# A new order of the engines' instruction streams, searched with other transfer times, in a fused linear-attention and gated-FFN layer

## The chip, the cores and the metric

The kernel runs on one core of a Trainium2 chip. The metric is the device time of one execution in microseconds (us). A core has a matrix engine (PE; its weight loads are listed apart as PEld), three engines for elementwise work (DVE, ACT, POOL), and SP, which in this kernel issues DMA transfers alone. Each engine runs its own instruction stream in the order in which it was written; between engines, semaphores make an instruction wait for what it needs.

## The reference

One layer for 2048 tokens of width 640, in bf16: linear attention with 32 heads of 20 on a layer-normed input, a residual, then a gated FFN without a nonlinearity on the layer-normed sum, a residual.

```python
def _A_ref(x, wqkv, w_phi, wo):
    qkv = (x @ wqkv).reshape(B, S, 3, H, Dh)  # to q, k, v per head
    pq = jnp.einsum("bhsd,hdf->bhsf", q, w_phi)
    pk = jnp.einsum("bhsd,hdf->bhsf", k, w_phi)
    phi_q = jnp.concatenate([_softmax(pq), _softmax(-pq)], axis=-1)
    phi_k = jnp.concatenate([_softmax(pk), _softmax(-pk)], axis=-1)
    kv = jnp.einsum("bhsf,bhsd->bhfd", phi_k, v)
    z  = jnp.einsum("bhsf->bhf", phi_k)
    num = jnp.einsum("bhqf,bhfd->bhqd", phi_q, kv)
    den = jnp.einsum("bhqf,bhf->bhq", phi_q, z)[..., None] + 1e-6
    return (num / den).reshape(B, S, D) @ wo

def _B_ref(x, w_gate, w_up, w_down):        # F = 1536
    return ((x @ w_gate) * (x @ w_up)) @ w_down

h = x + _A_ref(_layernorm(x), A_wqkv, A_w_phi, A_wo)
h2 = h + _B_ref(_layernorm(h), B_w_gate, B_w_up, B_w_down)
```

## The kernel before, in words

The 2048 tokens are 16 tiles of 128 (numbers 0 to 15 in the names below), and four blocks of four tiles for the FFN. The program is a list of operations, each of which belongs to a named unit:

- `in`, `lT*`, `lx*`, `lwq`, `lwo`, `lg`, `lu`, `ld`: loads of x (transposed, L553, and plain, L549) and of the weights. `ld` is the load of w_down, 1.92 MB, into the space (vaug) that held the values.
- `wk`, `x*`, `wv`, `c*`, `wm`, `wq*`, `y*`: the weights of keys, values and queries are centred and multiplied with w_phi. For the keys, PE turns w_k in five pieces (L746), ACT (L803) and DVE (L806) copy the last turn out with the mean (DVE L775) taken off, and PE multiplies with the block matrix Phi (which DVE's and POOL's L636 build) in five units, x0 to x4.
- `s0, s2, s4, s8, s12`: sums and sums of squares of a batch of tokens for the layer norm (PE with 129 columns, DVE L698 and L702, POOL L707 to L718).
- `k*` and `K*`: scores of a tile of keys (PE), their maximum (DVE L925, L928), two exponentials (ACT L933), sums and reciprocals (DVE L947, L949), and the softmax product (POOL L950).
- `v*`: values (PE, ACT L956). `A*` and `Aout`: kv, summed over all tiles in PSUM, and its copy (DVE L1037, L1040).
- `q*` and `Q*`: the same for a tile of queries, with three buffers `eq` for the exponentials. Four exponentials (two for the first tiles), DVE L987 and L993, POOL L994 and L999, and then SP issues two transposing loads (L553) of the tile into phiqT, the first half of five pieces of 128 columns and the second of six. A buffer of `eq` is free for a later tile when both halves have landed.
- `n*`: numerators and denominators of a tile (PE), the division (DVE L1073, L1075) and the transposing of the result. `h*`: times wo, the residual and the second norm.
- `f b.ft.j`: one of twelve tiles of F, for block b: in the first block two products on PE, two copies by ACT (L1139, L1143) and a multiplication on POOL (L1145); in the later blocks a scheme with seven half products instead of eight (L1210), where PE goes on with a PSUM tile that ACT (L1220) or DVE (L1235, L1237) has copied in between.
- `d*` and `D*`: the down projections, the residual (DVE L1342) and the store.

What an engine does after what is not found by a scheduler at run time or at build time. `ORDER` (L74 and following) holds for each of the five engines a list of unit names, and each name takes the next operation of that unit on that engine. `Prog.place()` walks the five lists at once with a model of the time of each operation (`t`: how long it holds its engine, `lat`: until its result can be used, `size`: a transfer's time on the DMA engines), takes at each step the operation that can start first, and gives out PSUM buffers (four of two banks, `ps`), the three `eq` buffers and the slots of the DMA rings in that order. `finish()` then writes the semaphore waits. The model's times thus don't run on the chip; they decide which buffer number an operation gets and in which order buffers come free, and they are what the lists were searched with.

Of the kernel before, what the change touches and what calls it, by code (L numbers as in the profile page):

```python
# [11 lines left out]
P = 128  # L12
S = 2048
D = 640
NT = S // P
NC = D // P
# [81 lines left out]
    "DVE":  # L98
# [16 lines left out]
    "ACT":  # L115
# [318 lines left out]
def _build(ctx, nc, A_x, A_wqkv, A_w_phi, A_wo, B_w_gate, B_w_up, B_w_down, out):  # L434
    g = Prog(nc, ctx)
# [8 lines left out]
    x_all = sb([P, NT, D], BF16, "x_all")  # L444
# [186 lines left out]
    for a in range(NC):  # L631
        lo, hi = CH[a]
        n = hi - lo + 1
# [866 lines left out]
```

## Time and profile before

| | |
|---|---|
| median of three runs | 267.84 us (267.67, 267.84, 268.10) |
| the profiled execution | 267.55 us |
| its span, first to last instruction | 265.8 us |
| mean granted clock of PE | 0.999 |
| instructions PE, DVE, ACT, POOL | 2418, 417, 387, 243 |
| DMA moved in the span | 28.65 MB |

The profile page gives the busy time of each engine, the span in slices, the chain of waits that ended last, and groups of instructions by line; the trace behind it answers for any window. A row of a timeline is: start in us, length in us, engine, line, operation, output and inputs with their shapes, how many in a row, and in brackets the idle time ahead and what ended it. The end of a matmul is modelled, so rows of PE overlap a little.

### The profile page before, as it was taken

What the parts mean: (1) busy time and instruction counts of PE and PEld (TensorE: products, weight loads), DVE (VectorE), ACT (ScalarE), POOL (GpSimd) and SP (SyncE); (2) the same over time, 40 slices, a digit from 0 to 9 for tenths busy, and PEclk for the clock granted to TensorE, in tenths of its full rate; (3) what the DMA queues carried; (4) which work ended last, traced back from release to release, by engine and by line L of the source; (5) the groups of instructions that cost most, each with busy time, mean ns of one, the idle gap of its engine ahead of it and who ended that gap; (6) DMA issues with size and microseconds to landing.
All of it is one profiled execution on the core that took longest, in us unless ns stands there. A gap on an engine that the chain in (4) does not pass through costs nothing.

```text
span 265.8 us, 6243 instructions
## 1 busy us (share of the span) xinstructions
PE 260.4 (98%) x2418; PEld 200.0 (75%) x2433; DVE 222.7 (84%) x417; ACT 177.2 (67%) x387; POOL 190.1 (72%) x243
## 2 busy tenths in 40 slices
PE   8999999999999999999999999999999999999995
PEld 8877777776877787777767887777777777777773
DVE  1999999999999876998999778988778788675683
ACT  2567999999857998769553695764857555645220
POOL 5446989999932889999974789359866575648652
PEclk9999999999999999999999999999999999999999
DMA  7997999903155789666856515300410401001012
GB/s 188 302 138 175 165 233 401 382 32 75 39 82 100 89 247 210 130 106 133 131 115 128 47 25 79 99 4 0 56 45 19 83 0 52 1 2 51 14 65 71
DMA packets 67390, 28.65 MB, mean 108 GB/s; under 512 B 57632, under 2 KB 66080, under 8 KB 67360
## 3 DMA queue, kind: packets, MB, share of 16 engines
q1 hardware_dynamic: 66432, 27.90, 48.7%
q10 hardware_dynamic: 928, 0.35, 0.5%
q8 instruction: 19, 0.31, 0.5%
q14 instruction: 11, 0.09, 0.1%
HBM read 11.82 MB, written 2.62 MB: 54 GB/s over the span
## 4 chain that ended last, share of the span: by engine, by line
PE 85%; DVE 5%; DMA 3%; ACT 3%; issue 1%; POOL 1%; SPq 0%; ACTq 0%
PE ps L657 60%; PE ps L1210 24%; DMA phiqT<-eq 3%; ACT eq L933 1%; DVE ob L1075 1%; PE ps L746 1%; DVE x_all L1093 1%; DVE ps L925 1%; DVE Sq L987 1%; ACT phiqT L1335 0%; POOL eq L999 0%; DVE rden L1073 0%; DVE phiqT L806 0%; ACT junk L650 0%; ACT eq L1220 0%
## 5 line engine op out<-in xcount | busy, mean ns | idle before, releaser
L657 PE MATMUL ps<-Wp,xT 128*128 128x320 bf16 (+1 forms) x606 | 89.1, 299 | 0.0
L657 PEld LDWEIGHTS ps<-Wp,xT 128*128 128x128 bf16 x606 | 58.0, 98 | 22.5 <-ACT phik L933 0.3
L1240 POOL TENSOR_TENSOR phik<-phik,gate 128x512 bf16<-128x512 bf16 x34 | 40.1, 1184 | 25.9 <-DVE phik L1237 25.5
L1220 ACT ACTIVATE eq<-ps 128x256 f32<-128x256 f32 x110 | 37.4, 386 | 23.0 <-PE ps L1210 18.6
L1210 PE MATMUL ps<-phik,Wgu 128*128 128x256 bf16 (+1 forms) x214 | 46.6, 299 | 0.2
L950 POOL TENSOR_TENSOR phik<-phik,Rk 128x1280 bf16<-128x1280 bf16 x16 | 37.4, 2357 | 5.8 <-DVE Rk L949 4.8
L657 PE MATMUL ps<-phik,Wgu 128*128 128x256 bf16 (+1 forms) x259 | 33.2, 280 | 0.1
L657 PEld LDWEIGHTS ps<-phik,Wgu 128*128 128x128 bf16 x260 | 25.0, 98 | 5.5
L1337 POOL TENSOR_TENSOR phiqT<-phiqT,x_all 128x320 f32<-128x320 f32 x26 | 21.7, 844 | 9.7 <-ACT phiqT L1335 9.6
L925 DVE TENSOR_REDUCE ps<-ps 128x1 f32<-128x640 f32 (+1 forms) x32 | 26.1, 818 | 2.8 <-PE ps L657 2.8
L1210 PEld LDWEIGHTS ps<-phik,Wgu 128*128 128x128 bf16 x228 | 21.9, 98 | 5.7 <-ACT eq L1220 0.2
L657 PE MATMUL ps<-vaug,phik 128*128 128x63 bf16 (+1 forms) x308 | 25.9, 238 | 0.0
L987 DVE TENSOR_REDUCE Sq<-eq 128x66 f32<-128x1320 bf16 x16 | 24.2, 1513 | 1.4 <-ACT eq L933 1.4
L1237 DVE TENSOR_TENSOR phik<-ps,eq 128x512 bf16<-128x512 f32 x28 | 19.1, 687 | 6.3 <-PE ps L1210 6.2
L1335 ACT ACTIVATE phiqT<-ps 128x320 f32<-128x320 f32 x26 | 11.4, 437 | 19.3 <-PE ps L657 19.2
L947 DVE TENSOR_REDUCE Ssum<-phik 128x64 f32<-128x1280 bf16 x16 | 23.3, 1460 | 0.0
L1235 DVE TENSOR_TENSOR gate<-ps,eq 128x512 bf16<-128x512 f32 x27 | 18.5, 685 | 5.2 <-PE ps L1210 2.9
L657 PEld LDWEIGHTS ps<-vaug,phik 128*128 128x128 bf16 x308 | 18.1, 97 | 5.3
L999 POOL TENSOR_TENSOR eq<-eq,rq 128x660 bf16<-128x660 bf16 x16 | 20.9, 1305 | 0.8
L933 ACT ACTIVATE eq<-ps,nb,rs 128x300 bf16<-128x300 f32 (+2 forms) x26 | 17.2, 689 | 6.1 <-DVE nb L928 4.5
L1342 DVE TENSOR_TENSOR outb<-ps,phiqT 128x320 bf16<-128x320 f32 x28 | 13.4, 487 | 6.9 <-PE ps L657 5.5
L1139 ACT ACTIVATE gate<-ps 128x256 bf16<-128x256 f32 (+1 forms) x26 | 10.4, 406 | 10.3 <-PE ps L657 9.6
(168 smaller groups left out, 526.2 us busy)
## 6 DMA issues: line engine op xcount, KB each, us to landing
x_all<-in_A_x_dram SPq DMA_DIRECT2D x4, 640.0 KB, 10.7
out_dram<-outb SPq DMA_DIRECT2D x14, 160.0 KB, 1.9
Wgu<-in_B_w_gate_dram SPq DMA_DIRECT2D x1, 1920.0 KB, 10.6
Wgu<-in_B_w_up_dram SPq DMA_DIRECT2D x1, 1920.0 KB, 16.3
vaug<-in_B_w_down_dram SPq DMA_DIRECT2D x1, 1920.0 KB, 8.5
Wp<-in_A_wqkv_dram SPq DMA_DIRECT2D x1, 800.0 KB, 5.0
phiqT<-in_A_wqkv_dram SPq DMA_DIRECT2D x1, 800.0 KB, 6.4
Wo<-in_A_wo_dram SPq DMA_DIRECT2D x1, 800.0 KB, 6.0
```

The lines of the kernel that those rows point to most:

```text
L657: ins = e.matmul(o_, lhsT=l_, rhs=r_, start=s_, stop=p_, skip_group_check=True)
L925: g.op("DVE", lambda e: e.tensor_reduce(out=mx(), in_=src(), axis=AX.XY if len(src().shape) == 3 else AX.X, op=ALU.max, apply_absolute_val ...
L933: g.op("ACT", lambda e, s=s, sc=sc, to=to, of=of: e.activation(out=to(s), in_=of(), func=ACT.Exp, bias=nb[:, i:i + 1], scale=sc[:, t:t + 1 ...
L947: g.op("DVE", lambda e: e.tensor_reduce(out=Ssum[:, vs.i, :], in_=x, axis=AX.X, op=ALU.add), rd=R_phik[t], wr=vs.R, use=[vs], t=1.39, lat=1.5)
L950: g.op("POOL", lambda e: e.tensor_tensor(out=x, in0=x, in1=Rk[:, vr.i, :].unsqueeze(2).to_broadcast([P, 2 * H, DH]), op=ALU.mult), rd=vr.R ...
L987: g.op("DVE", lambda e: e.tensor_reduce(out=Sq[:, vs.i, :].rearrange("p (w g) -> p w g", w=NQ), in_=feat(0, NQ).rearrange("p w (g f) -> p ...
L999: return e.tensor_tensor(out=x, in0=x, in1=rq[:, vr.i, :].rearrange("p (w h) -> p w h", h=HW).unsqueeze(3).to_broadcast([P, NQ, HW, DH]), ...
L1210: ins = e.matmul(o_, lhsT=l_[0](c), rhs=m_, start=fr, stop=False, skip_group_check=True)
L1220: g.op("ACT", lambda e: e.activation(out=half(s[i], 256 * h, 256 * (h + 1)), in_=PS[v.i][:, bk, 256:512], func=ACT.Copy), rd=[v.R[bk]], wr ...
L1237: g.op("DVE", lambda e: e.tensor_tensor(out=hhT[:, hb_, ft, :], in0=PS[v.i][:, 1, :], in1=half(s[1]), op=ALU.add), rd=[v.R[1]] + s[1].R, w ...
L1240: g.op(eng, lambda e: e.tensor_tensor(out=hhT[:, hb_, ft, :], in0=hhT[:, hb_, ft, :], in1=gate[:, vg.i, :], op=ALU.mult), rd=R_out + vg.R, ...
L1337: g.op("POOL", lambda e: e.tensor_tensor(out=slot(x), in0=slot(x), in1=x_all[:, t, c], op=ALU.add), rd=x.R + [R_h[t]], wr=x.R, use=[x], t= ...
```

## The change

The five lists in `ORDER` are replaced by others with the same names and the same number of each. Besides, some of the model's times are other numbers: a plain load is taken to be usable 0.6 us after its data instead of 1.9, a transposing load takes 0.45 us of the DMA engines instead of 1.07, the two halves of a query tile hold SP for 1.3 us and the DMA engines for 0.5, and so on. No operation is added, removed or changed.

```diff
 ORDER = {
     "PE":
-        "warm wk wk wk wk wk wk wk wk wk s0 wk x1 s0 x1 x3 wv wv x2 x0 x0 s2 x4 s2 k0 k0 k0 k0 k0 k3 k1 wm k2 v2 v3 s4 s4 s4 s4 "
+        "warm wk wk wk wk wk wk wk wk wk wk x1 s0 s0 x1 x3 x2 wv wv x0 x0 s2 x4 s2 k0 k0 k0 k0 k0 k3 k1 wm k2 v3 v2 s4 s4 s4 s4 "
...
     def load(out_, in_, wr, mb, eng="SP", at=0.0):
-        return g.op(eng, lambda e: e.dma_start(out_, in_), wr=wr, dma=("w", 8), t=0.5, lat=0.4 if at else 1.9, size=mb / 0.38, at=at)
+        return g.op(eng, lambda e: e.dma_start(out_, in_), wr=wr, dma=("w", 8), t=0.5, lat=0.4 if at else 0.6, size=mb / 0.38, at=at)
-    def transpose(out_, in_, rd, wr, use=(), t=1.27, size=1.07, lat=0.5, at=0.0):
+    def transpose(out_, in_, rd, wr, use=(), t=1.27, size=0.45, lat=0.3, at=0.0):
...
-                      b.R + [R_pad], [R_phiqT[bb][k][tt]], [b], t=0.254 * (w1 - w0), size=0.214 * (w1 - w0)))
+                      b.R + [R_pad], [R_phiqT[bb][k][tt]], [b], t=1.3, size=0.5, lat=0.35))
...
-            g.op("PE", f, ..., t=0.125 if act else 0.282, lat=0.275 if act else 0.43)
+            g.op("PE", f, ..., t=0.19 if act else 0.282, lat=0.34 if act else 0.43)
...
-    load(Wo[:, :, 0:D], A_wo.rearrange("(c p) n -> p c n", p=P), R_Wo, 1.5)
+    load(Wo[:, :, 0:D], A_wo.rearrange("(c p) n -> p c n", p=P), R_Wo, 0.95)
```

The lists tell little by themselves; three places in the built program show what moves. On PE, at the start of the program, where the turns of w_k (L746), the statistics s0 (128x129) and the products with Phi (128x140 and 128x80, six for a unit) alternate:

```order
 L746 MATMUL ps<-ident,phiqT 128x128 x5
 L657 MATMUL ps<-ones,phiqT 128x1 x5
-L657 MATMUL ps<-xT 128x129 x5
 L746 MATMUL ps<-ident,phiqT 128x128 x5
 L657 MATMUL ps<-Phi,phiqT 128x140 x2
 L657 MATMUL ps<-Phi,phiqT 128x80 x2
 L657 MATMUL ps<-Phi,phiqT 128x140 x2
-L657 MATMUL ps<-xT 128x129 x5
+L657 MATMUL ps<-xT 128x129 x10
 L657 MATMUL ps<-Phi,outb 128x140 x2
```

The fifth turn of w_k now comes ahead of the first five statistics matmuls, and these stand with the next five behind the first Phi unit. On DVE the last L636 goes ahead of the mean L775 there, and further on PE does x2 ahead of wv.

On SP, in the middle of the program, where the transposed halves of query tiles 7 (the first two rows), 4 and 6 stand with the load of w_down (vaug<-in_B_w_down_dram):

```order
 L553 DMA_TRANSPOSE phiqT<-eq 128x5x128
 L553 DMA_TRANSPOSE phiqT<-eq 128x6x128
+L549 DMA vaug<-in_B_w_down_dram 128x12x640
 L553 DMA_TRANSPOSE phiqT<-eq 128x5x128
-L549 DMA vaug<-in_B_w_down_dram 128x12x640
 L553 DMA_TRANSPOSE phiqT<-eq 128x6x128
 L553 DMA_TRANSPOSE phiqT<-eq 128x5x128
```

The load moves ahead of the first half of tile 4; before, it stood between the two halves.

On ACT, at query tile 10, whose four exponentials write an `eq` buffer (L1139 and L1143 are the copies of one FFN tile). Before:

```order
L933 ACTIVATE eq<-ps3,nb,rs 128x5x3x20
L933 ACTIVATE eq<-ps3,nb,rs 128x6x3x20
L933 ACTIVATE eq<-ps3,nb,nrs 128x5x3x20
L1139 ACTIVATE gate<-ps1 128x256
L933 ACTIVATE eq<-ps3,nb,nrs 128x6x3x20
L1143 ACTIVATE phik<-ps1 128x256
```

And after:

```order
L933 ACTIVATE eq<-ps1,nb,rs 128x5x3x20
L933 ACTIVATE eq<-ps1,nb,rs 128x6x3x20
L933 ACTIVATE eq<-ps1,nb,nrs 128x5x3x20
L933 ACTIVATE eq<-ps1,nb,nrs 128x6x3x20
L1139 ACTIVATE gate<-ps3 128x256
L1143 ACTIVATE phik<-ps3 128x256
```

The four stand together, and the buffer numbers of PSUM are others. On POOL the FFN multiplication `f0.0.0` goes ahead of query tile 4 and `f0.4.0` behind it; before, they stood the other way round. On PE the down projection `d1` goes ahead of `n6`. In the FFN of the later blocks neighbours change places.

More of the change, by code (lines that the diff above doesn't have):

```diff
@@ L587, in load_xT @@
     def load_xT(t, at=0.0):
-        transpose(lambda: xT[:, t, :, 0:P], lambda: A_x[0, P * t:P * (t + 1), :], [], [R_xT[t]], t=1.5, size=0.75, lat=1.25 if at else 2.75, at=at)
+        transpose(lambda: xT[:, t, :, 0:P], lambda: A_x[0, P * t:P * (t + 1), :], [], [R_xT[t]], t=1.5 if at else 1.4, size=0.75 if at else 0.62, lat=1.25 if at else 2.1, at=at)
     def load_x(b):
-        load(x_all[:, 4 * b:4 * b + 4, :], A_x[0, 4 * P * b:4 * P * (b + 1), :].rearrange("(t p) n -> p t n", p=P), [R_x[b]], 1.2)
+        load(x_all[:, 4 * b:4 * b + 4, :], A_x[0, 4 * P * b:4 * P * (b + 1), :].rearrange("(t p) n -> p t n", p=P), [R_x[b]], 0.9)
     def load_wv(c0, c1, at):
@@ L686, in f @@
                 return mms(e, lst)
-            g.op("PE", f, rd=[R_xT[t], R_one, R_xone], wr=[v.R[j // 2]], use=[v], t=0.125 if act else 0.282, lat=0.275 if act else 0.43)
+            g.op("PE", f, rd=[R_xT[t], R_one, R_xone], wr=[v.R[j // 2]], use=[v], t=0.19 if act else 0.282, lat=0.34 if act else 0.43)
             if act:
@@ L818, in wq_means @@
         v = Buf(p_ps, 2)
-        g.op("PE", lambda e: mms(e, mean_mms(PS[v.i][:, 0, :], range(NC), 0)), rd=R_Wnat + [R_one], wr=v.R, use=[v], t=0.64, lat=0.79)
+        g.op("PE", lambda e: mms(e, mean_mms(PS[v.i][:, 0, :], range(NC), 0)), rd=R_Wnat + [R_one], wr=v.R, use=[v], t=0.73, lat=0.88)
         g.op("ACT", lambda e: e.activation(out=nmeanq[:, :], in_=PS[v.i][:, 0, 0:NC], func=ACT.Copy, scale=-1.0 / SC),
@@ L1371, in wqT @@
         U("t%d" % a)
-        transpose(lambda: WT[:, 0, a, :], lambda: A_wqkv[:, P * a:P * (a + 1)], [], [R_WT[0][a]], t=1.5, size=0.75, lat=2.75)
+        transpose(lambda: WT[:, 0, a, :], lambda: A_wqkv[:, P * a:P * (a + 1)], [], [R_WT[0][a]], t=1.4, size=0.62, lat=2.1)
     U("warm")
```

122 rows, old and new, of the table ORDER are left out of this document.

## The prediction

> **What bounds the kernel now.** I read the busy times and the table of windows first, then the chain of waits, then the timeline of PE at each place where the chain leaves PE, and at last the engine that PE waits for there.
>
> The first line of the page, and rows of the windows (start:end and length, then busy time and count of PE, PEld, DVE, ACT, POOL, then clock, DMA share, GB/s):
>
> ```profile
> PE 260.4 (98%) x2418; PEld 200.0 (75%) x2433; DVE 222.7 (84%) x417; ACT 177.2 (67%) x387; POOL 190.1 (72%) x243
> ...
> 40.00:60.00 20.00, 20.00 (x157) 14.28 (x155) 20.00 (x32) 18.99 (x30) 19.46 (x19) 1.00 0.72 268
> 60.00:80.00 20.00, 19.71 (x303) 15.46 (x302) 19.26 (x39) 15.67 (x29) 15.51 (x12) 1.00 0.39 67
> 80.00:100.00 20.00, 19.90 (x205) 16.19 (x204) 17.12 (x30) 17.82 (x43) 13.07 (x23) 1.00 0.71 149
> 100.00:120.00 20.00, 19.78 (x180) 14.98 (x179) 17.09 (x34) 14.51 (x32) 18.70 (x29) 1.00 0.84 145
> 140.00:200.00 60.00, 59.63 (x495) 45.86 (x501) 50.54 (x94) 38.33 (x104) 43.05 (x55) 1.00 0.30 52
> ```
>
> PE is busy nearly all the time at full clock, and the same matmuls run before and after the change. So only PE's holes can be won, and they are few: 0.29 of 20 us, 0.10, 0.22. From 40 to 60 DVE is full too and POOL nearly: a lead that PE brings into this stretch lasts only if DVE and POOL bring it as well. After 140 the holes make 0.37 us in 60.
>
> The chain of waits (start, length, what) leaves PE at these places, among others:
>
> ```profile
> 7.95 1.07 DVE phiqT L806 x3
> 9.01 0.08 DVE sm L698
> ...
> 9.14 28.33 PE ps L657 x289
> ...
> 93.47 0.58 SPq L549
> ...
> 94.10 8.54 DMA phiqT<-eq
> ```
>
> At 9.14 PE waits for DVE, and near 105 for a chain that begins on SP's queue with a transposing load of a query tile and the load of w_down (L549).
>
> PE's own rows at the holes (in brackets: idle time and releaser), some with the row ahead or behind:
>
> ```profile
> 8.45 0.48 PE L657 MATMUL ps<-Phi,outb 128*128 128x140 bf16 x6
> 9.14 0.47 PE L657 MATMUL ps<-Phi,phiqT 128*128 128x140 bf16 x6 [0.21 <-DVE sm L698]
> ...
> 74.87 0.53 PE L657 MATMUL ps<-Phi,phiqT 128*128 128x42 bf16 x12 [0.29 <-DVE Phi L1040]
> ...
> 80.20 1.26 PE L657 MATMUL ps<-Wo,phik 128*128 128x320 bf16 x8
> 81.56 0.51 PE L657 MATMUL ps<-Phi,phiqT 128*128 128x63 bf16 x11
> ...
> 105.25 0.51 PE L657 MATMUL ps<-Phi,phiqT 128*128 128x63 bf16 x11 [0.22 <-ACT eq L933]
> 105.59 0.71 PE L657 MATMUL ps<-Wp,xT 128*128 128x300 bf16 x4
> ```
>
> Where PE doesn't wait, a row starts before the last one's end: 105.25 + 0.51 = 105.76, and the next starts at 105.59, 0.17 earlier. So the true hole is the idle time plus about 0.16: 0.37 at 9.14, 0.45 at 74.87, 0.10 + 0.16 = 0.26 at 81.56 (80.20 + 1.26 = 81.46), 0.38 at 105.25.
>
> **The change part by part.** The counts of operations stay, and the numbers given to the planner are not executed; only the order costs or gains. I go through the holes.
>
> *The start.* The rows of DVE, ACT and PE that make the hole at 9.14:
>
> ```profile
> 7.18 0.44 PE L657 MATMUL ps<-xT 128*128 128x129 bf16 x5
> 7.44 0.32 DVE L636 TENSOR_TENSOR Phi<-Wrows,G 128x160 bf16<-128x160 bf16 x1
> 7.46 0.44 PE L746 MATMUL ps<-ident,phiqT 128*128 128x128 bf16 x5
> 7.94 1.05 ACT L803 ACTIVATE phiqT<-ps,nmean 128x384 bf16<-128x384 bf16 x2 [0.80 <-PE ps L746]
> ```
>
> Five statistics matmuls (7.18) stand ahead of the fifth turn of w_k (7.46), which releases ACT's L803 and DVE's L806; from start to start they take 7.46 - 7.18 = 0.28. The change puts them behind that turn. DVE's third L636 (0.32) goes ahead of the mean L775 and ends before the turn does, so L806 starts 0.28 earlier, x3 too: 0.28 of the 0.37. The last 0.09 stays, since PE has the same work ahead of x3. x2 now runs before wv, which I count as 0.03 lost to the order of its neighbours. Taken: -0.25; bounds 0 and -0.37.
>
> Does it last? POOL is full from the statistics s8 until the third query tile:
>
> ```profile
> 37.54 0.22 POOL L708 TENSOR_SCALAR vpe<-sxx 128x4 f32<-128x4 f32 x1 [0.53 <-DVE sxx L702]
> ...
> L950 POOL TENSOR_TENSOR phik<-phik,Rk 128x1280 bf16<-128x1280 bf16 x11 | 25.7, 2357 | 0.0
> ...
> 72.73 1.31 POOL L999 TENSOR_TENSOR eq<-eq,rq 128x660 bf16<-128x660 bf16 x1
> ...
> 79.82 0.90 ACT L933 ACTIVATE eq<-ps,nb,rs 128x660 bf16<-128x660 f32 x1 [0.35 <-DMA phiqT<-eq]
> ```
>
> POOL's stretch begins with a wait for DVE, and DVE's keys follow PE from 10 us on, so POOL starts about 0.25 earlier as well, does the same eleven multiplications, and ends at 72.73 + 1.31 = 74.04 less 0.25. Its tile goes through SP and a transpose to ACT's wait at 79.82, which sets PE's hole at 81.56. So what the new order does to PE between 36 and 61 brings nothing to the end: at 81.56 PE's lead is cut back to POOL's 0.25. The wait at 74.87 is for DVE's copies of kv; nothing is placed differently there.
>
> *The load of w_down.* SP's rows, the times to landing, and ACT and DVE up to the hole:
>
> ```profile
> 89.53 3.89 SPq L553 DMA_TRANSPOSE phiqT<-eq  x2
> ...
> L553 SPq DMA_TRANSPOSE phiqT<-eq x2: 1276/1924/2573, 89.5 to 92.2; - x2
> ...
> DMA to landing us min/median/max: 2.7/3.4/4.1
> ...
> vaug<-in_B_w_down_dram SPq DMA_DIRECT2D x1, 1920.0 KB, 8.5
> ...
> 101.84 0.16 DVE L928 TENSOR_TENSOR nb<-ps,rs 128x1 f32<-128x1 f32 x1
> ...
> 102.74 1.14 ACT L933 ACTIVATE eq<-ps,nb,rs 128x300 bf16<-128x300 f32 x2 [0.84 <-DMA phiqT<-eq]
> 104.26 0.39 ACT L1139 ACTIVATE gate<-ps 128x256 bf16<-128x256 f32 x1
> 104.53 0.67 ACT L933 ACTIVATE eq<-ps,nb,nrs 128x360 bf16<-128x360 f32 x1
> 105.06 0.40 ACT L1143 ACTIVATE phik<-ps 128x256 bf16<-128x256 f32 x1
> ```
>
> The two transposes of the first row end at 89.53 + 3.89 = 93.42, and the second of them, 1.28 long, is the first half of query tile 4: issued at 92.15, landing at 92.15 + 2.7 = 94.85; the load is issued at 93.47 and lands at 93.47 + 8.5 = 101.97; the second half lands at 94.10 + 8.54 = 102.64, that is 0.67 behind the load. Only then may ACT overwrite the buffer that both halves read: its four exponentials of q10 run from 102.74 to 105.20 and release n4 on PE at 105.25. Now the load goes first, at 92.15: 93.47 - 92.15 = 1.32 earlier, landing at about 100.65, and both halves follow. At 0.67 each the second lands at 101.99, 0.65 earlier. DVE's value for q10 comes at 101.84 + 0.16 = 102.00, so not much more could be used. ACT's four exponentials now also stand together, without L1139 (104.53 - 104.26 = 0.27) ahead of the last. n4's release comes 0.9 earlier, where 0.38 is enough; the next, q14, waits for the L1143 that ends at 105.46, now 104.81, wanted at 105.59 - 0.38 = 105.21. So the hole of 0.38 closes. Were the landing to stay, only 0.04 would come of the 0.27, since q14 would wait for the same 105.46 (105.59 moves by at most 0.13, less what a release takes). Bounds: 0 and -0.38, and a loss if the halves come late (below). On POOL the product of tile 4 now stands behind the FFN's f0.0.0, which it was ahead of, and ends later, but SP too reaches the first half 0.6 later, after the load's issue.
>
> The Trainium skill, "DMA: Bandwidth & Descriptors", section on queues, rings and completion order, says that each of the 16 engines takes a ring's descriptors in order and that a completion count lands after all earlier writes. By that rule the first half, which now lands at 94.85, could not land before the whole load of 1920 KB, and moving a large load ahead of small transposes speaks against the change; the 0.67 by which the second half followed the load agrees with it.
>
> *From 113 on.* d1 goes ahead of n6, and small swaps follow in the FFN. Where a difference of two tiles is copied by ACT (L1220) before PE goes on with it, the waits view has this:
>
> ```profile
> PEld ps L1210 <- ACT eq L1220: 0.8, 4, 0.2
> ```
>
> That is 0.8 us in all in four waits, 0.2 each. In the new order three turns have as few matmuls between as the tightest now, and two others have more. The balance is one more, 0 to +0.2. Taken: +0.1; bounds -0.4 (the two) and +0.6 (the three). The end, from the last down projection to the store, is the same.
>
> *Sum.* -0.25 (start) - 0.38 (n4) + 0.1 (FFN) = -0.53, from which I take back 0.08, because the second half may land later than at the best. That is -0.45. The profiled execution took 267.55 us, its span 265.8, and the median of three runs is 267.84, 0.29 above it; the difference of -0.45 is made against the profile (267.10) and carried to the median: 267.4.
>
> **The rivals.**
>
> *Capped (267.6).* The second half of tile 4 lands no earlier, because the DMA engines have as much to move as before; then only the start is won, 267.84 - 0.25. For it: the order of the same transfers does not change their sum. Against it: in the windows the engines had idle time before the load's bulk, so an earlier issue has something to fill:
>
> ```profile
> 92.00:94.00 2.00, 2.00 (x21) 1.79 (x19) 2.00 (x2) 2.00 (x7) 0.52 (x2) 1.00 0.81 157
> 94.00:96.00 2.00, 2.00 (x28) 1.83 (x27) 1.26 (x4) 2.00 (x6) 1.97 (x4) 1.00 0.70 97
> 96.00:101.50 5.50, 5.50 (x58) 4.70 (x56) 4.11 (x7) 5.28 (x15) 5.25 (x11) 1.00 1.09 351
> ```
>
> The idle shares are 2 x 0.19 + 2 x 0.30 = 0.98 us, the most that can be won there.
>
> *Slower (268.65).* The two halves behind the load cost more than 0.67 each. A half by itself took 2.7 from issue to landing. With 2.7 for one and 0.67 for the other the second lands at 100.65 + 3.37 = 104.02; n4 follows 2.56 - 0.27 later (105.20 - 102.64 = 2.56) at about 106.3 instead of 105.25: +1.05, less 0.25 won at the start, +0.8. With 2.7 for both it would be 2.7 more. It decides when the second half lands after 102.64 + 0.27 = 102.91. For it: the first half landed 2.7 after its issue with no such load ahead. Against it: 0.67 was seen behind the same load.
>
> *All (266.6).* Besides, the 0.26 at 81.56 and the 0.37 between 140 and 200 go: 267.84 - 0.28 - 0.38 - 0.26 - 0.37 = 266.55. Against it: POOL and the transposes bound the first of these.
>
> *Nothing (267.8).* The start's 0.25 is lost in 40:60, where DVE has no idle time at all and a few swaps of its long reductions may cost as much.
>
> **How the numbers follow.** Chances: the forecast 0.45, capped 0.17, slower 0.19, all 0.14, nothing 0.05. About 0.2% (0.54 us) is what a measurement here can tell from no change, so under 267.30 is faster and over 268.38 slower. The forecast lies just inside and spreads by 0.3 (the FFN's bounds and the 0.38), so about 0.23 of its 0.45 is faster, and all of "all": 0.37. Slower keeps 0.18, the rest is 0.45. The range takes in "all" and most of "slower": 266.6 to 268.6.
>
> **What would show it.** Right: x3 at about 8.86 without most of the idle time, POOL's third query tile ending near 73.8, the load of w_down landing near 100.4 and the second half of tile 4 before 102.1, no wait of PE at n4, the span near 265.35. Wrong: the transposes behind the load landing after 102.9, a PE hole at n4 of a microsecond, new waits of PE on ACT's L1220 that add up to more than 0.6, or PE's lead gone by 60 us.

## The result, and the profile after

The changed kernel took 269.11 us in the median of ten executions (268.34 to 270.35), the kernel before 267.61 on the same chip (267.04 to 268.19). The ratio is 1.0064, with a 95% interval from 1.0043 to 1.0086: slower by 0.6%, where 267.4 was forecast. The profiled execution took 269.03 us, its span 267.3 at a granted clock of 0.999; the span of before was 265.8, so the 1.5 us lie in the span and not in the clock. The ratios here and below leave out executions that are over 1.5% longer than the fastest of their kernel and have a lower granted clock; among the changed kernels that is one execution, of the kernel with the load alone moved (272.18 us, granted 0.994).

From the page of after, the busy times and the chain that ended last:

```profile
PE 261.3 (98%) x2433; PEld 199.7 (75%) x2433; DVE 224.2 (84%) x417; ACT 178.1 (67%) x387; POOL 189.8 (71%) x243
...
PE 63%; POOL 15%; DVE 9%; DMA 5%; SPq 4%; ACT 2%; issue 1%; ACTq 0%; DVEq 0%
...
vaug<-in_B_w_down_dram SPq DMA_DIRECT2D x1, 1920.0 KB, 9.3
```

The shares of busy time look as they did. (PE's 0.9 us more is no added work: the trace of before lacks 15 matmul records, 2418 against 2433.) The windows show where PE now has holes, in the same columns as for before:

```profile
100.00:120.00 20.00, 19.88 (x181) 15.27 (x180) 18.17 (x32) 15.24 (x33) 18.85 (x29) 1.00 0.74 118
120.00:140.00 20.00, 19.39 (x178) 14.02 (x176) 16.93 (x32) 13.94 (x29) 17.41 (x20) 1.00 0.70 123
```

From 100 to 120 the holes shrink from 0.22 to 0.12 us; from 120 to 140 they make 0.61, in a stretch that the prediction had shown no window of. After the one from 40 to 60 it was the fullest one of before:

```profile
120.00:140.00 20.00, 19.95 (x183) 14.74 (x183) 18.29 (x35) 13.83 (x27) 17.82 (x21) 1.00 0.70 127
```

PE's own rows of after at the places that matter:

```profile
9.44 0.85 PE L657 MATMUL ps<-Wp,ones 128*128 128x320 bf16 x5
...
80.95 0.50 PE L657 MATMUL ps<-Phi,phiqT 128*128 128x63 bf16 x11
...
83.78 0.51 PE L657 MATMUL ps<-Phi,phiqT 128*128 128x63 bf16 x11 [0.34 <-ACT eq L933]
...
104.82 0.50 PE L657 MATMUL ps<-Phi,phiqT 128*128 128x63 bf16 x11
...
113.15 0.72 PE L657 MATMUL ps<-phik,Wgu 128*128 128x256 bf16 x5
...
133.27 0.50 PE L657 MATMUL ps<-Phi,phiqT 128*128 128x63 bf16 x11
133.61 0.71 PE L657 MATMUL ps<-phik,Wgu 128*128 128x256 bf16 x5
134.84 1.53 PE L657 MATMUL ps<-Wo,phik 128*128 128x320 bf16 x10 [0.52 <-DVE phik L1148]
...
167.01 1.53 PE L657 MATMUL ps<-Wo,vaug 128*128 128x320 bf16 x10 [0.36 <-DVE phik L1237]
```

And rows of before at n3, f0.7.2 and h10:

```profile
83.86 0.49 PE L657 MATMUL ps<-Phi,phiqT 128*128 128x63 bf16 x11
...
113.29 0.71 PE L657 MATMUL ps<-phik,Wgu 128*128 128x256 bf16 x5
...
134.05 1.53 PE L657 MATMUL ps<-Wo,phik 128*128 128x320 bf16 x10
```

Read as after less before, row by row: PE is 0.61 us ahead at 80.95 (n2, 81.56 before), 0.08 at 83.78 (n3), 0.43 at 104.82 (n4, 105.25 before), 0.14 at 113.15 (f0.7.2), and then behind: 0.79 at 134.84 (h10, 134.05 before). Two holes make the turn: 0.25 ahead of n11 at 133.27, and 0.52 + 0.16 = 0.68 ahead of 134.84; two of 0.16 follow by 137. That is 1.26 us in four microseconds, where before had 0.08. At 167.01 another 0.36 + 0.16 = 0.52 opens (h15). So -0.14 + 1.18 + 0.52, less 0.06 in small ones, gives the 1.50 by which the last matmul comes later.

The first two of these holes go back to SP. Its rows from 112 to 121 us, before and after (n6 is the vaug<-ob; the two or three phiqT<-eq behind it begin with query tile 14's):

```profile
114.84 1.20 SPq L553 DMA_TRANSPOSE vaug<-ob  x1
116.39 4.62 SPq L553 DMA_TRANSPOSE phiqT<-eq  x3
```

```profile
90.54 0.58 SPq L549 DMA_DIRECT2D vaug<-in_B_w_down_dram  x1
93.24 4.55 SPq L553 DMA_TRANSPOSE phiqT<-eq  x2
...
114.41 1.28 SPq L553 DMA_TRANSPOSE vaug<-ob  x1
118.22 3.85 SPq L553 DMA_TRANSPOSE phiqT<-eq  x3
```

Before, SP stood still for 116.39 - 116.04 = 0.35; after, for 118.22 - 115.69 = 2.53. POOL says why. Its softmax products of query tiles (L999), before and after:

```profile
115.06 1.30 POOL L999 TENSOR_TENSOR eq<-eq,rq 128x660 bf16<-128x660 bf16 x1
...
117.10 1.31 POOL L999 TENSOR_TENSOR eq<-eq,rq 128x660 bf16<-128x660 bf16 x1
```

```profile
91.58 0.26 POOL L994 TENSOR_TENSOR rq<-Sq,rq 128x33 f32<-128x33 f32 x1 [1.07 <-DVE rq L993]
91.91 1.30 POOL L999 TENSOR_TENSOR eq<-eq,rq 128x660 bf16<-128x660 bf16 x1
...
115.62 2.57 POOL L999 TENSOR_TENSOR eq<-eq,rq 128x660 bf16<-128x660 bf16 x2
```

Before, POOL made tile 14 (to 116.36) and then tile 9 (to 118.41), the order in which SP sends them. The new list of POOL has tile 9 first (to 116.93) and tile 14 second (to 118.19), but SP's list still sends tile 14 first. So tile 9 lies ready for 1.3 us behind an issue that waits for tile 14. What follows on SP are issues of 1.28 us each without a gap, all about 1.05 late; the second half of tile 11 lands at 133.18 instead of 132.04. n11 needs that half, and ACT's exponentials of q13 need its buffer:

```profile
133.29 0.60 ACT L933 ACTIVATE eq<-ps,nb,rs 128x300 bf16<-128x300 f32 x1 [1.06 <-DMA phiqT<-eq]
```

The copy of the FFN tile f0.8.2 (L1139, from 133.79) stands behind them on ACT, DVE's L1148 waits for it, and PE's h10 for that:

```profile
134.26 0.42 DVE L1148 TENSOR_TENSOR phik<-ps,gate 128x256 bf16<-128x256 f32 x1 [0.82 <-ACT gate L1139]
```

A second swap of the same kind shows in SP's rows near 91: 93.24 - 91.12 = 2.12 us of waiting for query tile 4, between the early load and its first half. POOL's L994 waited 1.07 there for DVE. DVE after:

```profile
90.33 0.16 DVE L1104 TENSOR_TENSOR nmh<-ps,mv 128x1 f32<-128x1 f32 x1 [1.02 <-PE ps L657]
90.41 0.81 DVE L1107 TENSOR_TENSOR x_all<-ps,x_all 128x640 bf16<-128x640 f32 x1
91.14 0.35 DVE L993 RECIPROCAL rq<-Sq 128x33 f32<-128x33 f32 x1
```

and DVE and POOL before:

```profile
89.61 0.37 DVE L993 RECIPROCAL rq<-Sq 128x33 f32<-128x33 f32 x1
...
90.40 1.31 POOL L999 TENSOR_TENSOR eq<-eq,rq 128x660 bf16<-128x660 bf16 x1
```

The reciprocal of tile 4 (0.35 us) now stands behind the residual of h2, which waits for PE. It starts 1.53 later, and tile 4 is ready at 93.22 instead of 91.71.

### The profile page after: what moved, and what is told of

It reads as the page before. It is cut to its first block, busy times and chain, and to the rows that moved or that the text cites. A ratio compares the mean times of both kernels' runs of the same rounds, so it can differ in the third digit from the quotient of the medians.

```text
span 267.3 us, 6254 instructions
## 1 busy us (share of the span) xinstructions
PE 261.3 (98%) x2433; PEld 199.7 (75%) x2433; DVE 224.2 (84%) x417; ACT 178.1 (67%) x387; POOL 189.8 (71%) x243
## 3 DMA queue, kind: packets, MB, share of 16 engines
HBM read 11.82 MB, written 2.62 MB: 54 GB/s over the span
## 4 chain that ended last, share of the span: by engine, by line
PE 63%; POOL 15%; DVE 9%; DMA 5%; SPq 4%; ACT 2%; issue 1%; ACTq 0%; DVEq 0%
PE ps L657 42%; PE ps L1210 20%; POOL phik L950 7%; SPq L553 3%; DMA phiqT<-eq 3%; DVE Ssum L947 2%; POOL eq L999 2%; POOL phik L1240 2%; DVE ps L925 2%; DMA phiqT<-in_A_wqkv_dram 2%; DVE Rk L949 1%; ACT eq L933 1%; DMA phik<-hb 1%; POOL Wp L1164 1%; ACT junk L650 1%
## 5 line engine op out<-in xcount | busy, mean ns | idle before, releaser
L1240 POOL TENSOR_TENSOR phik<-phik,gate 128x512 bf16<-128x512 bf16 x34 | 40.4, 1193 | 23.9 <-DVE phik L1237 23.4
L1220 ACT ACTIVATE eq<-ps 128x256 f32<-128x256 f32 x110 | 37.6, 386 | 21.2 <-PE ps L1210 16.3
L1210 PE MATMUL ps<-phik,Wgu 128*128 128x256 bf16 (+1 forms) x228 | 50.4, 304 | 0.0
L657 PE MATMUL ps<-phik,Wgu 128*128 128x256 bf16 (+1 forms) x260 | 33.3, 281 | 0.1
L999 POOL TENSOR_TENSOR eq<-eq,rq 128x660 bf16<-128x660 bf16 x16 | 20.8, 1306 | 0.9
L1139 ACT ACTIVATE gate<-ps 128x256 bf16<-128x256 f32 (+1 forms) x26 | 10.4, 403 | 11.2 <-PE ps L657 6.6
```

The source lines that it names most:

```text
L657: ins = e.matmul(o_, lhsT=l_, rhs=r_, start=s_, stop=p_, skip_group_check=True)
L999: return e.tensor_tensor(out=x, in0=x, in1=rq[:, vr.i, :].rearrange("p (w h) -> p w h", h=HW).unsqueeze(3).to_broadcast([P, NQ, HW, DH]), ...
L1210: ins = e.matmul(o_, lhsT=l_[0](c), rhs=m_, start=fr, stop=False, skip_group_check=True)
L1220: g.op("ACT", lambda e: e.activation(out=half(s[i], 256 * h, 256 * (h + 1)), in_=PS[v.i][:, bk, 256:512], func=ACT.Copy), rd=[v.R[bk]], wr ...
L1240: g.op(eng, lambda e: e.tensor_tensor(out=hhT[:, hb_, ft, :], in0=hhT[:, hb_, ft, :], in1=gate[:, vg.i, :], op=ALU.mult), rd=R_out + vg.R, ...
```

## The experiments

The theory after the traces: each stream of orders is fine by itself, but POOL makes query tiles in another order than SP sends them, and SP issues in order. The rivals: the early load of w_down costs on its own, through what its data do to the transposes (as the prediction's "Slower"); and the model's numbers, which give other PSUM buffers, cost by themselves. All kernels were timed in five rounds beside the kernel before; ratios are to that, on the same chip. The experiments ran on four chips, so it is their ratios that compare with one another. Names stand for the next operation of that unit on the engine.

**POOL's order of tiles 14 and 9, alone, both ways.** First put back in the changed kernel:

```diff
 POOL (after)
-h7 Q14 h5 h7 Q9 Q14 h5 h7 h5
+h7 Q14 h5 Q14 h7 h7 Q9 h5 h5
```

> The changed kernel with one thing put back: on POOL the product of query tile 14 stands ahead of that of tile 9 again, as SP's list has their transposes. Theory (SP stands still): SP doesn't wait 2.5 us for tile 14 at 115.7, its queue runs 1 us earlier, the landing of tile 11 at 133.2 and with it PE's holes between 132.9 and 136.9 (1.26 us) go, and perhaps the one at 166 (0.5): about 1.2 to 1.8 us faster than the changed kernel, 267.3 to 267.9, the same as before within 0.2%. Rival (the order of DVE and ACT around tile 13 and FFN tile f0.8.2, or the buffers given out): the holes stay, 269.0.

Measured: 268.31 (267.24 to 269.37), ratio 1.0018, interval 1.0001 to 1.0035. SP's rows of this kernel:

```profile
115.43 1.28 SPq L553 DMA_TRANSPOSE vaug<-ob  x1
117.08 4.19 SPq L553 DMA_TRANSPOSE phiqT<-eq  x3
```

The stop is 117.08 - 116.71 = 0.37 again, and the holes at 133 to 137 are gone. Two others opened ahead of them, where SP was held during the load: 0.35 at n4 and 0.43 at f0.7.2; so the time was above the 267.3 to 267.9 that were expected. Still, about 0.46% of 0.64% comes back with one swap on POOL. The wait at h15 is gone too, although POOL's order behind 140 us is still that of the changed kernel:

```profile
166.53 1.53 PE L657 MATMUL ps<-Wo,vaug 128*128 128x320 bf16 x10
```

Then the swap put into the kernel before:

```diff
 POOL (before)
-h7 Q14 h5 Q14 h7 h7 Q9 h5 h5
+h7 Q14 h5 h7 Q9 Q14 h5 h7 h5
```

> The kernel before with only that swap on POOL: the product of tile 9 ahead of that of tile 14, SP's list as it was. Theory (SP stands still): SP waits about 2 us for tile 14 instead of 0.4, its queue is late by 1 us or more, and PE gets holes of about 1 us near 133 to 137: 268.6 to 269.2. Rival (DVE, ACT or the buffers): no change, 267.6.

Measured: 268.87 (268.41 to 269.25), ratio 1.0044, interval 1.0031 to 1.0057. SP and PE of this kernel:

```profile
114.59 1.20 SPq L553 DMA_TRANSPOSE vaug<-ob  x1
117.97 3.85 SPq L553 DMA_TRANSPOSE phiqT<-eq  x3
```

```profile
134.60 1.53 PE L657 MATMUL ps<-Wo,phik 128*128 128x320 bf16 x10 [0.52 <-DVE phik L1148]
```

The stop (2.18) and the wait at h10, to its length and its releaser, are those of after. The swap alone makes 1.2 us of the loss, with the old load and the old start. This cause is shown from both sides.

**SP's order instead of POOL's.** In the changed kernel, SP sends tile 9 first:

```diff
 SP (after)
-n6 Q14 Q14 Q9 Q9 n8
+n6 Q9 Q9 Q14 Q14 n8
```

> The changed kernel with SP's list brought to POOL's instead: the halves of tile 9 ahead of those of tile 14. Theory (SP stands still for a tile that POOL makes later): SP waits for tile 9 until 116.9 and not for tile 14 until 118.2, so half of the 2.5 us goes and the queue is 1.2 us earlier; PE's holes at 133 to 137 shrink from 1.26 to 0.3 or less: 268.0 to 268.5. Rival (it is POOL's order as such): 269.0.

Measured: 268.39 (267.40 to 270.15), ratio 1.0033, interval 1.0016 to 1.0050. The holes from 133 to 136 shrink from 1.26 to 0.49 us, where 0.3 or less was expected. So bringing the two lists into agreement from SP's side helps as well. Whether it helps as much as POOL's old order isn't shown, since the intervals of the two kernels overlap.

**The start, alone,** put into the kernel before (with the moves on DVE and POOL that go with it):

```diff
 PE (before)
-wk wk s0 wk x1 s0 x1 x3 wv wv x2 x0
+wk wk wk x1 s0 s0 x1 x3 x2 wv wv x0
```

> The kernel before with only the new order of its first 12 us on PE, DVE and POOL. Theory: PE's hole at 9 us is cut and PE is 0.2 us ahead until a wait for a transposed tile near 81 or 113 cuts it back: between 0 and -0.25, 267.4 to 267.6. Rival (the lead lasts to the end): -0.25. Rival (a lead changes which waits come last later, either sign): over 0.5 either way.

Measured: 267.27 (266.90 to 267.66), ratio 0.9977, interval 0.9959 to 0.9995. In its trace PE is 0.25 us ahead from 34 to 80 us, 0.13 to 0.21 from 82 to 98, and 0.34 from n4 (105) to the end. The theory, a lead cut back at n3, missed; its rival, a lead that lasts to the end, came true. By the interval this part of the change is worth 0.13 to 1.1 us, and the prediction's 0.25 lies within.

**The load ahead of tile 4, alone,** put into the kernel before:

```diff
 SP (before)
-Q7 Q7 Q4 ld Q4 Q6
+Q7 Q7 ld Q4 Q4 Q6
```

> The kernel before with only the load of w_down ahead of both halves of query tile 4. Theory: the second half lands a microsecond earlier, PE's hole of 0.38 at n4 closes, but the first product of f0.7.2 waits for a transposed tile of SP's queue that is still bound by POOL's tile 6 and by 1.28 us for each issue, so the gain ends at 113: 0 to -0.15, 267.5. Rival (what closes at n4 stays won): -0.38, 267.2. Rival (the transposes behind the load come late): slower by over 0.5.

Measured: 268.43 (267.06 to 269.61) in the eleven executions that count, ratio 1.0025, interval 1.0003 to 1.0047; 267.5 was expected. Its profiled execution (267.60) shows n4's hole closed, with the second half landing at 101.95, and no loss in the middle. What makes others of its executions up to 2.0 us longer than this one isn't in a trace, so that stays open. What the trace does show is SP: with tile 4 ready, its first half held SP for 3.95 us and its second for 2.88, where before only the second half was held (3.51).

**Both put back in the changed kernel,** POOL's order and the load between the halves:

```diff
 POOL as in the first experiment, and SP (after)
-Q7 Q7 ld Q4 Q4 Q6
+Q7 Q7 Q4 ld Q4 Q6
```

> The changed kernel with both suspects put back: tile 14 ahead of tile 9 on POOL, and the load of w_down between the halves of tile 4 on SP. Theory (the loss is SP's standing still for tile 14 and SP's being held while the load drains; the rest of the new order is worth the start's 0.2 to 0.4): 267.2 to 267.6, ratio 0.997 to 1.000, and times as close together as those of the kernel before. Rival (the rest of the new order costs too): 268.0 or more.

Measured: 268.96 (268.04 to 269.32), ratio 1.0051, interval 1.0037 to 1.0065: slower than with the load left early, and the theory's figure is missed. PE of this kernel at n4:

```profile
105.45 0.51 PE L657 MATMUL ps<-Phi,phiqT 128*128 128x63 bf16 x11 [0.73 <-ACT eq L933]
```

A hole of 0.73 + 0.16 = 0.89 at a place that should have been as before. Its cause is in the DVE rows shown above: tile 4 is ready late, SP stands still for 1.73 us, and with the load back behind the first half, the load and the second half are late too. In the changed kernel the early load fills that stop. The theory as it stood knew one reversal; there were two.

**The model's numbers alone,** with the lists of before; from the middle of the program on, operations get other PSUM buffers:

```diff
-... lat=0.4 if at else 1.9, size=mb / 0.38, at=at)
+... lat=0.4 if at else 0.6, size=mb / 0.38, at=at)
...
-... t=1.27, size=1.07, lat=0.5, at=0.0):
+... t=1.27, size=0.45, lat=0.3, at=0.0):
```

> The kernel before with the planner's new numbers alone, its five lists as they were: the same order on every engine, other PSUM buffers from the middle of the program on. Theory (the lists make the difference): 267.5 to 267.9, no change. Rival (which buffer an operation gets moves the waits): over 0.5 us either way.

Measured: 267.60 (267.10 to 267.79), ratio 1.0005, interval 0.9996 to 1.0014. No change: this rival is out.

**The load behind both halves,** with the start, in the kernel before:

```diff
 SP (before, with the new start)
-Q7 Q7 Q4 ld Q4 Q6
+Q7 Q7 Q4 Q4 ld Q6
```

> The kernel before with the new start and with the load of w_down behind both halves of tile 4. Theory (the load holds SP's next transposes, whichever they are): PE's hole at n4 closes, since both halves land by 96.5; SP is held at tile 6 instead, by no more than before, and POOL's T0 waits up to 1.5 us for the load. The start's gain stays, and nothing more than it can pass f0.7.2: 267.1 to 267.4. Rival (tile 6 lands late and q9 waits for it): 267.8 or more.

Measured: 267.88 (267.29 to 268.89), ratio 1.0015, interval 1.0005 to 1.0026. The second half lands at 95.89 and n4's hole is gone, but holes of 0.27 at 95.3 and 0.16 at 109.5 and three that add up to 0.54 from 134.1 to 136.1 (0.08 there before) stand in its place. The theory's 267.1 to 267.4 is missed, and the rival's figure (267.8 or more) is met: closing n4's hole that way gives back more than it wins.

**DVE's reciprocal, alone,** moved in the kernel before:

```diff
 DVE (before)
-q8 Q4 q8 Q4 h2 h2 h3
+q8 Q4 q8 h2 h2 Q4 h3
```

> The kernel before with one thing of the new order: on DVE the reciprocal of tile 4 (L993, 0.36 us) behind the two operations of h2 that wait for PE. Theory: the reciprocal starts at 91.1 instead of 89.6, POOL's product ends at 93.2 instead of 91.7, SP stands still for 1.0 to 1.5 us before tile 4 with the load behind it, the second half lands near 103.8, and PE's hole at n4 grows from 0.4 to 1.0 to 1.6: 268.3 to 268.9. Rival (SP's queue makes it up, since the load lands when it lands): 267.5 to 267.8.

Measured: 268.97 (268.80 to 269.29), ratio 1.0051, interval 1.0038 to 1.0064. SP and PE of this kernel:

```profile
88.39 6.36 SPq L553 DMA_TRANSPOSE phiqT<-eq  x3
94.79 0.58 SPq L549 DMA_DIRECT2D vaug<-in_B_w_down_dram  x1
```

```profile
106.59 0.51 PE L657 MATMUL ps<-Phi,phiqT 128*128 128x63 bf16 x11 [1.29 <-ACT eq L933]
```

The load is issued at 94.79 instead of 93.47, the second half lands at 103.97 instead of 102.64, and n4 waits 1.29 + 0.16 = 1.45 us. One instruction of 0.35 us, moved behind two that wait for PE, costs 1.3 us, just above what was expected. The reciprocal starts at 91.43 instead of 89.61, 1.82 later. The three transposes shown as one row include a stop of SP of 2.62, longer than the 1.0 to 1.5 that the theory asked for; the first half's issue comes 1.40 later (93.55 instead of 92.15), which is in that range.

**Three reversals put back in the changed kernel:** POOL's tiles 14 and 9, the load between the halves, and tile 4 ahead of h2 on DVE and ahead of f0.0.0 on POOL:

```diff
 DVE (after)
-Q4 h2 h2 Q4 h3 h3
+Q4 Q4 h2 h2 h3 h3
 POOL (after), besides the swap of tiles 14 and 9
-f0.10.0 f0.0.0 Q4 Q4 f0.4.0 h2
+f0.10.0 f0.4.0 Q4 Q4 f0.0.0 h2
 SP (after)
-Q7 Q7 ld Q4 Q4 Q6
+Q7 Q7 Q4 ld Q4 Q6
```

> The changed kernel with three things put back: tile 14 ahead of tile 9 on POOL, the load of w_down between the halves of tile 4 on SP, and tile 4 itself early again (on DVE its reciprocal L993 ahead of the two operations of h2 that wait for PE, on POOL its product ahead of f0.0.0). Theory (each tile that DVE or POOL brings late makes SP, which takes its list in order, stand still): SP doesn't stand still for 1.7 us at 91, tile 4's second half lands at about 102.3, PE's holes at n4 (1.1 us with that at 106) and at f0.7.2 (0.27) shrink to 0.4 or less: 267.3 to 267.7. Rival (something else in the new order costs): 268.4 or more, as with only two of them back.

Measured: 267.72 (266.99 to 268.58), ratio 1.0004, interval 0.9992 to 1.0016. The loss is gone. With what remains, the start among it, the profiled execution is 0.93 us ahead of before at h10 (133.12) and 0.76 near 141; at h15, where PE waits, 0.52 are left, and 0.35 at the end:

```profile
165.16 1.53 PE L657 MATMUL ps<-Wo,vaug 128*128 128x320 bf16 x10 [0.36 <-DVE phik L1237]
```

**The same with the load left early:**

```diff
 SP (three put back)
-Q7 Q7 Q4 ld Q4 Q6
+Q7 Q7 ld Q4 Q4 Q6
```

> The changed kernel with tile 14 and tile 4 early again on POOL and DVE, and the load of w_down left where the change put it, ahead of both halves of tile 4. It differs from the kernel with three things back by the load alone. Theory (with tile 4 ready in time the load doesn't fill an idle SP any more but holds two transposes instead of one): 0.3 to 0.7 us slower than with three things back, 268.0 to 268.5, and times that lie further apart (over 2 us from end to end). Rival (the early load is worth what was forecast): 267.3 to 267.7.

Measured: 267.87 (267.17 to 269.44), ratio 1.0018, interval 1.0000 to 1.0036, which overlaps the last one's: whether the early load costs anything once tile 4 is in time is not settled. Its executions spread over 2.3 us, against 1.6 with the load between the halves. SP and PE of its profiled execution:

```profile
92.20 8.48 SPq L553 DMA_TRANSPOSE phiqT<-eq  x3
```

```profile
114.00 0.72 PE L657 MATMUL ps<-phik,Wgu 128*128 128x256 bf16 x5 [0.47 <-DMA phik<-hb]
```

Three issues, the two halves of tile 4 and the next one, hold SP for 8.48 us (3.34, 3.27 and 1.80); before, three such took 1.28 + 3.51 + 2.08. The transposing load of h2 lands at 113.95 instead of 113.23, and PE waits for it.

Four of these kernels are the changed one with POOL's tiles 14 and 9 put back; they differ in two things only, whether tile 4 is late or in time and where the load stands:

| | load ahead of both halves | load between the halves |
|---|---|---|
| tile 4 late | 1.0018 (1.0001 to 1.0035) | 1.0051 (1.0037 to 1.0065) |
| tile 4 in time | 1.0018 (1.0000 to 1.0036) | 1.0004 (0.9992 to 1.0016) |

With the load between the halves, the lateness of tile 4 costs 0.47%, 1.3 us, as it does in the kernel before. With the load ahead of them it costs nothing that these times show. So the early load is worth 0.33% while tile 4 is late, and nothing, or a small loss, once tile 4 is in time: the edit that the prediction counted on paid only for another part of the same change. The expectation for the last kernel (268.0 to 268.5) and its rival (267.3 to 267.7) both missed its time.

**POOL's order behind 140 us:** three back, and besides the list of POOL from h10 to h9 as before, which takes h10 and h9 forward:

```diff
 POOL (three put back)
-h10 h8 T3 G1.1 h8 h11 h10 T3 h11 h9 G2.1 h11 f1.1.0 G2.3 f1.3.0 h10 h14 h9 h9 G1.3
+h10 h8 T3 G1.1 h10 h11 h8 h11 T3 G2.1 h11 h9 f1.1.0 G2.3 f1.3.0 h10 h9 h14 h9 G1.3
```

> The changed kernel with three things back, and on POOL around 145 us the order of before for the small steps of h8 to h14 (0.6 us of work moves into an idle stretch ahead of h11). Theory (PE was 0.9 us ahead of the kernel before until h15, where POOL's full stretch from 150 to 165 cuts the lead back by 0.5): the hole at h15 shrinks by up to 0.5, 267.0 to 267.4. Rival (other waits bound h15): 267.7, no change.

Measured: 267.25 (266.98 to 268.30), ratio 0.9984, interval 0.9975 to 0.9992: faster than both kernels, by 0.16% than the one before. The row that waited in the kernel with three reversals put back no longer does:

```profile
166.30 1.53 PE L657 MATMUL ps<-Wo,vaug 128*128 128x320 bf16 x10
```

This profiled execution was the longest of its eleven, 268.30, and so the row stands later. Its start shows why; the load of the values' weights was late:

```profile
10.82 1.53 PE L657 MATMUL ps<-Wp,ones 128*128 128x320 bf16 x10 [1.38 <-DMA Wp<-in_A_wqkv_dram]
```

After, this unit started at 9.44 without idle time.

POOL's order is only part of what makes h15 wait. The first experiment keeps the changed order and has no wait there, nor have the two with SP's order or with two parts put back. On POOL the pair of L1240 ahead of h15 starts 27.33 us after h10 in this kernel, 27.41 before, 27.78 in the first experiment, 28.21 with three put back and 28.34 after. The changed order thus goes with about 0.45 us on POOL; the further 0.4 to 0.5 in the kernels where PE waits have no cause that the traces show. By the ratios this last edit is worth about 0.2%, 0.5 us, and its interval only touches that of the kernel without it (0.9992).

## Why the prediction was wrong, point by point

- **The start** was right. -0.25 was taken; PE starts x3 at 8.62 (8.86 was forecast) and the products behind the values at 12.50 instead of 12.71, 0.21 earlier; alone the start gives -0.23%. That it lasts through the full stretch of DVE and POOL, by POOL's own earlier start, held too: POOL's third product of a query tile ends at 73.67, where 73.8 was forecast.
- **The load of w_down** was right in its mechanism and wrong as a term of the sum. It was forecast to land at 100.65 and the second half at 101.99; they landed at 99.8 and 101.1, and n4's hole closed. That the landing fits so well is in part luck. The prediction had the load issued at 92.15, where the first half stood; but that place had waited for tile 4, which the load doesn't need, so it was issued at 90.54, 1.6 earlier, and then took 9.3 to land instead of 8.5. The transposing loads of after that were issued from 93.24 on:

```profile
L553 SPq DMA_TRANSPOSE phiqT<-eq x3: 1246/1699/3264, 93.2 to 97.9; - x3
...
DMA to landing us min/median/max: 3.7/6.6/7.2
```

  93.24 + 7.2 = 100.4 for the first half and 94.53 + 6.6 = 101.1 for the second, 0.6 and 0.7 one behind another, where 0.67 was taken. The rule of the Trainium skill, "DMA: Bandwidth & Descriptors", section on queues, rings and completion order, agrees: neither half landed ahead of the load, at 90.54 + 9.3 = 99.8. But -0.38 was added to the sum as though it reached the end. Of the 0.43 at 104.82, 0.14 are left at 113.15, since PE waits there for h2's landing, and SP sends back to back from 98 us on: that landing came at 113.11, and at 113.23 before. The lead at one hole was capped by the next on the same queue; the chain of after shows it:

```profile
109.28 1.11 SPq L553
110.43 2.67 DMA phik<-hb
113.15 20.03 PE ps L657 x182
```

- **Tile 4 on POOL**, the step that said its product "ends later, but SP too reaches the first half 0.6 later", failed. It weighed only POOL's own swap. DVE's reciprocal had moved as well, behind h2, and that made tile 4 1.5 us later: SP stood still for 2.12. Alone this move costs 1.3 us (1.0051); in the changed kernel the early load happens to fill the stop, which no term of the prediction stands for.
- **From 113 on**, the step that took +0.1 with bounds -0.4 and +0.6, failed, and this is most of the miss. What it counted came out within its bounds: PE waits for ACT's L1220 in three places, 0.2 each, one fewer than before where one more was forecast. What it called small swaps held the swap of tiles 14 and 9 on POOL (1.2 us): SP stood still for 2.53 us instead of 0.35, and PE had 1.26 us of holes from 133 to 137. They also held POOL's new order from h10 on, which has a part in the 0.52 at h15. The step went through PE's neighbours; it never set the order in which POOL and DVE make the tiles beside the order in which SP sends them.
- **The rivals.** "Slower" had the side and about half of the size (0.8 of the 1.50 measured), but not the mechanism: it decides at a landing after 102.91, and the landing was at 101.1. None of the rivals was a stop of SP for a tile that is made too late. "All" supposed that the hole at 81.56 could go; it went (0.61 ahead at 80.95), and nearly all of it was lost 2.8 us later at n3, where ACT waited for tile 3's second half. That wait is there in the traces in which SP's issue near 75 us, the second half of tile 2, took over 2.2 us (2.33 after), and absent in the three of the changed kernel's kind in which it took about 1.3. Why it takes longer in some isn't shown. Nor could "All" have won the 0.37 that it counted as holes between 140 and 200: the trace of before lacks 15 matmul records and shows as many idle bits of 0.05 us behind 137 us, 7 of them there, and the trace of after, which has all its records, shows none of them.
- **The signs.** Of those listed as signs of being right, all came true but the span, and none of those listed as signs of being wrong did: x3, POOL's tile, the landings of the load and of the second half and n4 all came out near the forecast. The list had no sign for an order of making against an order of sending, the step that failed.

In all: by its ratios the swap of tiles 14 and 9 costs 1.2 us either way; POOL's order from h10 on has a part in a wait of 0.5, and the intervals of the two kernels that tell it only touch; the start gives back 0.34 at the end of its trace and 0.6 by its ratio. Tile 4's lateness costs 1.3 us where the load stands between the halves, and nothing that the times show where the load stands ahead of them.

## What to carry to other kernels

Where one engine issues transfers in order and others make their contents, set the order of making beside the order of sending, tile by tile, before anything else is weighed: an item made out of turn stops the whole queue, and the length of the stop sets the price, not that of the instruction that was moved. A stop 1.8 us longer cost 1.2 us here, and an issue 1.4 later cost 1.3; idle time behind it can take up a part. Follow the lead that an edit wins to the next place that waits on the same queue; a queue that sends back to back takes it back there. Look through the busiest windows of before when an order changes, also those in which nothing was to be won: a new wait there has no idle time to hide in. And when several orders change at once, time them in pairs, since one part can pay only for what another one breaks.

## What the runs showed of the hardware

- In these traces the issue of a transposing load mostly held SP for 1.20 to 1.30 us, and some took 1.4 to 2.8 (2.15 at 103.10 before, 2.76 at 102.32 after). The longest came while the load of 1.92 MB drained: 3.51 for one issue before, 3.34 and 3.27 for two in a row that stood behind the load, 3.95 and 2.88 with the load alone moved. In the changed kernel only one was so long (3.26), since SP stood still for tile 4 through a part of that time.
- A transposing load mostly landed 2.6 to 2.9 us after its issue, and some over 4 (n6's: 4.28 before, 4.20 after; tile 11's second half: 4.36 and 4.45). In the 14 traces kept here, from 70 us on and away from the load of w_down, 89 of 703 transposing loads landed 4.0 us or more after their issue, and with every one of the 89 a packet of a DMA queue named "instruction" started between the issue and the landing (after: issue 114.41, packet 116.50, landing 118.6). Of the 492 that landed within 2.95, 53 had such a packet. No run tests whether the packet is the cause.
- One reciprocal of 0.35 us, moved by 1.8 (from 89.61 to 91.43), moved the first half's issue by 1.4 and the end by 1.3.
